# A head's products with v in two groups instead of three, and a pair's sums moved beside one of them

## The chip, the cores and the metric

The kernel runs on one core of one Trainium2 chip. The metric is the device time of one execution in microseconds (us). Before the change it is 525.54 us (median of three runs, 524.73 to 526.39).

## The reference

The program computes attention for 4 x 8 = 32 heads over 768 positions of width 64, with a mask: a key counts for a query only where both fall in the same bucket of 64 (the signs of six projections). The attention's output, seen as 3072 rows of width 512, goes through a soft mixture of 8 experts with 4 slots each.

```python
mask = q_bucket[:, :, :, None] == k_bucket[:, :, None, :]
scores = np.where(mask, scale * np.matmul(q, k.transpose(0, 1, 3, 2)), -1000000000.0)
attn = np.exp(scores - np.max(scores, axis=-1, keepdims=True))
attn = attn / (np.sum(attn, axis=-1, keepdims=True) + 1e-09)
x = np.matmul(attn, v)                  # rows of 512 = 8 heads x 64
logits = x @ phi                        # 32 slots
# softmax over rows feeds slots, w1, relu, w2; softmax over slots mixes them back
```

## The kernel before

**The work of a head.** Each head's 768 keys are six blocks of 128. For one head the kernel does the following.

- `smax` (L360): twelve products of 96 rows (L370), of 512 or 256 columns, whose row maxima VectorE takes (L373, L376). The twelve products fill nine PSUM tiles `smx` in turn: product n = 0 fills the first, 1 and 2 share the second, 3 the third, 4 the fourth, 5 and 6 the fifth, 7 the sixth, 8 the seventh, 9 and 10 the eighth, 11 the ninth. There are two buffers for them (L239), so a tile can be written once the maximum of the tile two before it has been taken. Here they are called M0 to M8.
- `shift` and `shift_rows` (L378, L389): three small VectorE steps make the shift from the maxima, TensorE transposes it (L404), ScalarE copies it (L407), and a DMA puts it into a row of the head's operands.
- `scores` (L411): twelve pairs of products (L421) into three PSUM buffers `st`, and an exponential on ScalarE (L425) into one of three tiles `pt`, one for each two blocks of keys.
- `acc` (L427): GpSimd adds up the exponentials of a head (L432, L438) for the sums.
- `av` (L440): the products with v. One call handles two blocks, with two halves of the columns side by side in the array, each 64 columns wide. One call is 4 products, which appear as 8 matmul records (L449). The third call of a head is followed by ScalarE's copy of the result to `avs` (L453).

**The work of a pair of heads.** `pair_sum` (L456) sums `acc` over the partitions with four products 32 columns wide (8 records, L461), and ScalarE copies the result to `sm` (L464). `pair_turn` (L492) transposes `sm` on TensorE (three transposes, L496); VectorE copies and inverts a small part (L498, L499). `pair_rec` (L466) inverts `sm` in place, a third at a time, on VectorE (L468); it overwrites what `pair_turn` reads, so it comes behind it. `pair_log` (L470) makes logits (8 records, L476), `pair_add` (L480) scales and adds them on VectorE (L488, L490), `pair_x` (L501) transposes and scales `avs` (L511, L513). On every second head VectorE also makes the low parts of the next pair's operands (`split_lo`, L292, two subtractions) and thresholds its bits (L321).

**What sets the order.** The order of the program is written out by hand. Every step gets a place on a line of slots, six slots a head, by the numbers in `WHEN` and `FIRST` (L45 to L113); the steps are sorted by it (L793) and written out in that order. Each engine runs its own instructions in the order in which they were written out. `pair_sum` of a pair has the number 16.448 counted from the start of the pair's first head, so it falls into the even head that comes after the pair. `s0` is the start of head h, `x` is 0 for even heads and 1 for odd ones.

Heads overlap: while the scores of head h run, the maxima of heads h + 1 and h + 2 are taken.

Of the kernel before, what the change touches and what calls it, by code (L numbers as in the profile page):

```python
# [17 lines left out]
BH = B * H  # L18
# [26 lines left out]
WHEN = {'load': -23.456,  # L45
 'bits': -14.465,
 'split_hi': -14.035,
 'split_lo': [-13.1, -12.626],
 'spread': [[-12.12, -11.747, -10.749, -7.5], [-12.05, -10.773, -10.639, -11.794]],
 'load_v': [-1.88, -1.85],  # L50
 'smax': [[-8.153, -7.646, -7.592, -7.407, -6.31, -6.263, -5.991, -5.086, -4.829, -4.442, -4.009, -3.019],
          [-7.926, -7.769, -7.645, -6.916, -6.247, -6.159, -6.133, -5.32, -4.829, -3.608, -3.608, -3.119]],
 'scores': [[-0.175, 0.609, 1.069, 1.557, 1.767, 2.599, 2.628, 3.37, 4.446, 4.862, 5.118, 5.577],
# [1 line left out]
 'shift': [-2.471, -2.398],  # L55
 'shift_rows': [-2.151, -1.917],
 'acc': [[5.646, 6.72, 8.258], [5.625, 6.02, 9.329]],
 'av': [[3.513, 6.554, 6.938], [3.513, 5.087, 6.68]],
 'pair_sum': 16.448,
 'pair_turn': 18.256,  # L60
 'pair_rec': [18.379, 18.389, 18.942],
 'pair_log': 18.557,
 'pair_x': [22.815, 24.33],
 'pair_add': 19.89,
# [83 lines left out]
def lsh_attention_soft_moe(  # L148
# [566 lines left out]
    def at(when, f, *args):  # L715
        key = (f.__name__, *(a for a in args if isinstance(a, int)))
        plan.append((FIRST.get(key, when), len(plan), (f, *args)))
# [10 lines left out]
    for h in range(BH):  # L728
        s0, x = NT * h, h % 2
        if x == 0:  # L730
            if h > 0:
                at(s0 + WHEN["load"], load, h)
            at(s0 + WHEN["bits"], bits, h)
            at(s0 + WHEN["split_hi"], split_hi, h)
            for n in range(2):
                at(s0 + WHEN["split_lo"][n], split_lo, h, n)
        for n, f in enumerate((spread_y, spread_bits, spread_l, spread_x)):
            at(s0 + WHEN["spread"][x][n], f, h)
        at(s0 + WHEN["load_v"][x], load_v, h)
        for n in range(2 * NT):  # L740
            at(s0 + WHEN["smax"][x][n], smax, h, n // 2, n % 2)
            at(s0 + WHEN["scores"][x][n], scores, h, n // 2, n % 2)
        at(s0 + WHEN["shift"][x], shift, h)
        at(s0 + WHEN["shift_rows"][x], shift_rows, h)
        for j in range(NT // 2):
            lone = h == BH - 1 and j == NT // 2 - 1
            at(s0 + (5.725 if lone else WHEN["acc"][x][j]), acc, h, j)
            if lone:
                for n in range(2):
                    at(s0 + 5.85 + n, av, h, j, n)  # L750
            else:
                at(s0 + WHEN["av"][x][j], av, h, j)
        if x and h < BH - 1:
            p, p0 = h - 1, s0 - NT
            at(p0 + WHEN["pair_sum"], pair_sum, p)
            at(p0 + WHEN["pair_turn"], pair_turn, p)
            for n in range(3):
                at(p0 + WHEN["pair_rec"][n], pair_rec, p, n)
            at(p0 + WHEN["pair_log"], pair_log, p)
            at(p0 + WHEN["pair_x"][0], pair_x, p, (0, 1))  # L760
            at(p0 + WHEN["pair_x"][1], pair_x, p, (2,))
            at(p0 + WHEN["pair_add"], pair_add, p)
        if h % H == H - 1 and h < BH - 1:
            for f in (batch_both, batch_max, batch_exp, batch_turn, batch_scale, batch_slots, batch_weigh, batch_share):
                at(p0 + WHEN[f.__name__], f, h // H)
    last, h = NT * BH, BH - 1
# [243 lines left out]
```

## Time and profile before

| What | Value |
|---|---|
| Time, median of three runs | 525.54 us |
| Profiled execution, its own time | 524.46 us |
| Its span from first to last instruction | 522.4 us |
| Granted TensorE clock, mean | 0.987 |
| TensorE busy | 499.2 us (96%) |
| VectorE busy | 369.3 us (71%) |
| GpSimd busy | 326.8 us (63%) |
| ScalarE busy | 246.6 us (47%) |
| Products with v (L449), busy | 145.3 us in 768 records |
| Row maxima (L376 and L373), busy | 130.8 and 65.6 us in 192 and 96 instructions |

A row of a timeline gives the start in us, the length in us, the engine, the line, the operation, what is written and read, the shape and how many instructions are merged. PE is TensorE, PEld its weight loads, DVE VectorE, ACT ScalarE, POOL GpSimd, SP the DMA issuing engine. Idle time before an instruction and what ended it stand in brackets. Two neighbouring rows can overlap, since an instruction's record reaches into the next one's; the distance between two starts is the time that the first one holds its engine.

### The profile page before, as it was taken

Reading aid. Unit: us, or ns where it says so; the run is one execution under the profiler, and the core shown is the slowest. Engines: PE = TensorE matmul, PEld = TensorE weight load, DVE = VectorE, ACT = ScalarE, POOL = GpSimd, SP = SyncE. Lnnn points to the kernel's source line nnn. Section 1 sums busy time; section 2 is a strip of 40 time slices with the busy share of each in tenths; the row PEclk is TensorE's granted clock in tenths of the full one; section 3 lists DMA queues with packets and bytes.
Section 4 is the critical chain, followed back from the end, with each engine's and each line's share of the span. In section 5 each row is a group of like instructions: output and inputs, shape, how many; then the busy total and the mean of one; then the engine's idle time right before and its main releaser. Section 6 shows DMA issues by size and latency. Waiting matters only on the chain.

```text
span 522.4 us, 9095 instructions
## 1 busy us (share of the span) xinstructions
PE 499.2 (96%) x3164; PEld 284.3 (54%) x3164; DVE 369.3 (71%) x703; ACT 246.6 (47%) x463; POOL 326.8 (63%) x223
## 2 busy tenths in 40 slices
PE   7968999999999999999999999999999999999992
PEld 4544555555555555556554555565555555553562
DVE  6574877787878787777787788787777885464233
ACT  4144536464646454545454545454644545422232
POOL 9246767676739776767488785856588767411200
PEclk9789999999999999999999999999999999999998
DMA  5747475758585657575765757676636366879967
GB/s 126 188 98 188 116 196 173 193 168 197 169 197 168 178 143 203 152 210 143 217 149 167 183 175 178 188 181 182 146 101 154 73 156 234 319 286 352 410 275 293
DMA packets 39777, 99.59 MB, mean 191 GB/s; under 512 B 7458, under 2 KB 13732, under 8 KB 39732
## 3 DMA queue, kind: packets, MB, share of 16 engines
q1 hardware_dynamic: 39540, 98.94, 66.3%
q8 instruction: 25, 0.41, 0.3%
q14 instruction: 20, 0.16, 0.1%
q0 software_dynamic: 192, 0.08, 0.1%
HBM read 52.76 MB, written 6.29 MB: 113 GB/s over the span
## 4 chain that ended last, share of the span: by engine, by line
PE 70%; DVE 10%; SPq 7%; DMA 6%; POOL 2%; issue 2%; ACT 1%; DVEq 0%; ACTq 0%; POOLq 0%
PE st L421 20%; PE av L449 19%; PE smx L370 13%; SPq L296 7%; DMA XY<-bt 4%; PE qs L933 3%; DVE w L292 3%; PE qh L851 3%; DVE mx L376 3%; PE mi L461 2%; PE mi L476 2%; POOL acc L438 1%; PE mi L328 1%; DMA w<-w 1%; DMA XY<-w 1%
## 5 line engine op out<-in xcount | busy, mean ns | idle before, releaser
L438 POOL TENSOR_TENSOR acc<-acc,pt 128x768 f32<-128x768 f32 x125 | 238.8, 1911 | 39.4 <-ACT pt L425 27.1
L425 ACT ACTIVATE pt<-st 128x512 f32<-128x512 f32 x288 | 162.0, 595 | 97.2 <-PE st L421 90.8
L421 PE MATMUL st<-XY 128*128 128x512 f32 (+1 forms) x768 | 183.7, 347 | 0.0
L376 DVE TENSOR_REDUCE mx<-smx 128x1 f32<-128x512 f32 x192 | 130.8, 687 | 54.1 <-PE smx L370 53.8
L449 PE MATMUL av<-pt,v 128*64 128x384 f32 x768 | 145.3, 499 | 0.0
L370 PE MATMUL smx<-XY 96*128 96x512 f32 (+1 forms) x384 | 126.6, 375 | 9.9 <-DVE mx L376 5.4
L421 PEld LDWEIGHTS st<-XY 128*128 128x128 f32 x768 | 123.7, 191 | 21.1 <-issue 10.6
L370 PEld LDWEIGHTS smx<-XY 96*128 96x128 f32 x384 | 70.1, 191 | 74.4 <-DVE mx L376 26.1
L432 POOL TENSOR_TENSOR acc<-pt 128x768 f32<-128x768 f32 x32 | 58.6, 1830 | 63.8 <-ACT pt L425 63.8
L449 PEld LDWEIGHTS av<-pt,v 128*64 128x64 f32 x768 | 46.5, 136 | 62.7 <-issue 57.5
L373 DVE TENSOR_REDUCE mx<-smx 128x2 f32<-128x512 f32 x96 | 65.6, 683 | 4.3 <-PE smx L370 4.1
L292 DVE TENSOR_TENSOR w<-raw,w 128x768 fp32r<-128x768 f32 x30 | 41.2, 1373 | 3.7 <-ACT w L288 3.7
L468 DVE RECIPROCAL sm<-sm 128x128 f32<-128x128 f32 x45 | 39.6, 910 | 0.0
L288 ACT CAST w<-raw 128x768 fp32r<-128x768 f32 x32 | 25.1, 831 | 19.5 <-DMA XY<-w 9.7
L453 ACT COPY avs<-av 128x384 f32<-128x384 f32 x32 | 15.3, 478 | 37.2 <-PE av L449 37.2
L407 ACT CAST mr<-mi 12x128 fp32r<-12x128 f32 x31 | 7.9, 255 | 49.2 <-PE mi L404 44.6
L321 DVE TENSOR_SCALAR bt<-mi,con 128x384 fp32r<-128x384 f32 x15 | 10.1, 677 | 25.3 <-DMA XY<-bt 9.6
L607 POOL TENSOR_TENSOR dl<-lacc,dl 64x384 f32<-64x384 f32 x3 | 3.0, 999 | 25.6 <-ACT dl L606 25.6
L513 DVE TENSOR_TENSOR xq<-mi,r 128x256 f32<-128x256 f32 x45 | 17.3, 412 | 0.4 <-PE mi L511 0.4
L328 PE MATMUL mi<-raw,pb 128*32 128x384 f32 x128 | 15.2, 517 | 0.1
L933 PE MATMUL qs<-w 128*32 128x256 f32 x232 | 15.2, 382 | 0.0
L511 PE MATMUL mi<-ident,avs 128*128 128x128 f32 x90 | 14.8, 273 | 0.0
(173 smaller groups left out, 339.4 us busy)
## 6 DMA issues: line engine op xcount, KB each, us to landing
w<-w SPq DMA_DIRECT2D x61, 512.0 KB
XY<-w SPq DMA_DIRECT2D x63, 384.0 KB
raw<-qk SPq DMA_DIRECT2D x32, 384.0 KB
XY<-w SPq DMA_DIRECT2D x64, 192.0 KB
v<-vt SPq DMA_DIRECT2D x32, 192.0 KB
out<-w SPq DMA_DIRECT2D x12, 512.0 KB
xq<-w SPq DMA_DIRECT2D x3, 512.0 KB
XY<-bt SPq DMA_DIRECT2D x62, 19.5 KB
```

The source lines that it names most:

```text
L292: (nc.vector if h else nc.gpsimd).tensor_tensor(out=w[:, 2 * x + 1], in0=st[h]["raw"][:, x], in1=w[:, 2 * x], op=ALU.subtract)
L296: eng.dma_start(out=dst.bitcast(F32), in_=src.bitcast(F32))
L370: nc.tensor.matmul(pt[:, o:o + b - a], s["Y"][0:96, 0, t * P:(t + 1) * P], s["Y"][0:96, 1, a:b], start=True, stop=True)
L373: nc.vector.tensor_reduce(out=mx[:, n - 1:n + 1], in_=pt.rearrange("p (a x) -> p a x", a=2), axis=AX.X, op=ALU.max)
L376: nc.vector.reduce_max(out=mx[:, n:n + 1], in_=pt, axis=AX.X)
L421: nc.tensor.matmul(pt[:, o:o + b - a], x[:, 1, i * P:(i + 1) * P], x[:, 0, a:b], start=first, stop=not first)
L425: nc.scalar.activation(s["P", i // 2][:, 512 * u:512 * u + 512], pt, AF.Exp, scale=D ** -0.5)
L432: nc.gpsimd.tensor_tensor(out=s["acc"], in0=pr[:, 0:S], in1=pr[:, S:2 * S], op=ALU.add)
L438: eng.tensor_tensor(out=s["acc"], in0=s["acc"], in1=pr[:, a * S:(a + 1) * S], op=ALU.add)
L449: nc.tensor.matmul(s["av"][64 * c:64 * c + 64, 0:HC], s["v"][:, i, :], pr[:, o + c * HC:o + (c + 1) * HC], start=(i == 0), stop=(i == NT - 1))
L468: nc.vector.reciprocal(out=rs[:, k * P:(k + 1) * P], in_=rs[:, k * P:(k + 1) * P])
L933: nc.tensor.matmul(po[32 * j:32 * j + 32], hTs[g][:, f, 32 * j:32 * j + 32], wt[1, x, 2 * g + f // 4, j][:, (f % 4) * HM:(f % 4 + 1) * HM] ...
```

## The change

The second and the third call of `av` of a head now stand directly behind each other, in even heads at the place of the former second call and in odd heads at the place of the former third, so 8 + 8 records become 16. The last head keeps its former numbers. `pair_sum` moves from the middle of an even head's score products to the place directly ahead of this group of 16; `pair_log` stands directly behind it, as it did behind the former second call. `pair_turn` moves from ahead of the second call to behind the first score products of the next head, and the three parts of `pair_rec` move behind it: the first ahead of the maximum of M5, the second and the third between the maxima of M5 and M6.

```diff
- 'av': [[3.513, 6.554, 6.938], [3.513, 5.087, 6.68]],
- 'pair_sum': 16.448,
- 'pair_turn': 18.256,
- 'pair_rec': [18.379, 18.389, 18.942],
+ 'av': [[3.513, 6.55, 6.555], [3.513, 6.67, 6.68]],
+ 'pair_sum': 18.5,
+ 'pair_turn': 18.9,
+ 'pair_rec': [18.91, 18.92, 18.95],
...
-                at(s0 + WHEN["av"][x][j], av, h, j)
+                at(s0 + (WHEN["av"][x][j] if h < BH - 1 else (3.513, 5.087)[j]), av, h, j)
```

The order on TensorE around the changed places, worked out from the numbers (`n` is the product of `smax`):

```
even head, before: scores, pair_sum, n=3, scores, n=4, n=5, n=6, pair_turn, av 2nd, pair_log, scores,
                   n=7, av 3rd, n=8, scores, n=9, scores, n=10, scores, n=11
even head, after:  scores, n=3, scores, n=4, n=5, n=6, pair_sum, av 2nd and 3rd, pair_log, scores,
                   pair_turn, n=7, n=8, scores, n=9, scores, n=10, scores, n=11
odd head, before:  n=3, av 2nd, n=4, scores, n=5, n=6, pair_x, scores, av 3rd, n=7
odd head, after:   n=3, n=4, scores, n=5, n=6, pair_x, scores, av 2nd and 3rd, n=7
```

On VectorE in the even head it was M4, turn, rec, rec, M5, rec, M6, add, M7, M8 and becomes M4, turn, rec, M5, rec, rec, M6, add, M7, M8 (the turn now a longer way behind M4). In the odd head VectorE's order stays as it was.

## The prediction

> **What bounds the kernel now.** I read the page first, then the busy time of one pair of heads, then the timelines of TensorE and VectorE through that pair, and last who waits for whom.
>
> ```profile
> span 522.4 us, 9095 instructions
> PE 499.2 (96%) x3164; PEld 284.3 (54%) x3164; DVE 369.3 (71%) x703; ACT 246.6 (47%) x463; POOL 326.8 (63%) x223
> ```
>
> TensorE looks like the whole bound. The middle of the kernel is 15 pairs of heads of about one length; one is cut out here by two starts of `pair_sum`. The columns are the stretch, its length, and the busy time of PE, PEld, DVE, ACT and POOL.
>
> ```profile
> 225.66:251.83 26.17, 26.17 (x157) 15.21 (x156) 20.21 (x38) 13.70 (x25) 18.91 (x11) 1.00 0.67 182
> ```
>
> TensorE has no gap in this pair, and the clock is fully granted. VectorE has 26.17 - 20.21 = 6.0 us to spare. That is little for an engine that TensorE leans on through only two buffers of maxima, so it matters where those 6.0 us lie. Here is TensorE's order through the even head, with what the change touches:
>
> ```profile
> 225.10 0.63 PE L421 MATMUL st<-XY 128*128 128x512 f32 x2
> 225.66 0.85 PE L461 MATMUL mi<-acc,ones 128*32 128x384 f32 x8
> 226.44 0.50 PE L370 MATMUL smx<-XY 96*128 96x512 f32 x1
> 226.78 1.10 PE L421 MATMUL st<-XY 128*128 128x256 f32 x6
> ...
> 228.19 0.49 PE L496 MATMUL mi<-ident,sm 128*128 128x128 f32 x3
> 228.61 1.51 PE L449 MATMUL av<-pt,v 128*64 128x384 f32 x8
> 230.05 0.85 PE L476 MATMUL mi<-avs,phs 64*32 64x384 f32 x8
> 230.83 0.73 PE L421 MATMUL st<-XY 128*128 128x512 f32 x2
> 231.40 0.40 PE L370 MATMUL smx<-XY 96*128 96x512 f32 x1
> 231.73 1.51 PE L449 MATMUL av<-pt,v 128*64 128x384 f32 x8
> 233.18 0.50 PE L370 MATMUL smx<-XY 96*128 96x512 f32 x1
> 233.51 0.63 PE L421 MATMUL st<-XY 128*128 128x256 f32 x4
> 233.99 0.28 PE L370 MATMUL smx<-XY 96*128 96x256 f32 x1
> ```
>
> The product n = 7 is at 231.40, n = 8 at 233.18 and n = 9 at 233.99. VectorE in the same stretch:
>
> ```profile
> 224.95 0.69 DVE L376 TENSOR_REDUCE mx<-smx 128x1 f32<-128x512 f32 x1 [0.95 <-PE smx L370]
> ...
> 229.36 0.16 DVE L498 COPY r<-mi 128x12 f32<-128x12 f32 x1
> ...
> 229.70 1.71 DVE L468 RECIPROCAL sm<-sm 128x128 f32<-128x128 f32 x2
> 231.84 0.69 DVE L376 TENSOR_REDUCE mx<-smx 128x1 f32<-128x512 f32 x1 [0.44 <-PE smx L370]
> 232.45 0.94 DVE L468 RECIPROCAL sm<-sm 128x128 f32<-128x128 f32 x1
> 233.71 0.69 DVE L376 TENSOR_REDUCE mx<-smx 128x1 f32<-128x512 f32 x1 [0.32 <-PE smx L370]
> 234.32 0.55 DVE L488 TENSOR_TENSOR sm<-mi,sm 128x384 f32<-128x384 f32 x1
> ...
> 235.38 0.68 DVE L373 TENSOR_REDUCE mx<-smx 128x2 f32<-128x512 f32 x1
> ...
> 236.79 0.17 DVE L382 TENSOR_REDUCE m<-mx 128x6 f32<-128x12 f32 x1
> ...
> 237.41 0.17 DVE L385 SCALAR_TENSOR_TENSOR mz<-m,mz 128x6 f32<-128x6 f32 x1
> ```
>
> The reader is to see that the copy of the turn and two reciprocals (229.36 to 231.41) run while TensorE is in its second group with v and the logits (228.61 to 230.83), where no maxima come in. M5, at 231.84, finds VectorE idle.
>
> **The gain on TensorE.** What a separate group costs is read from the third call of an even head. From n = 7 to the scores behind n = 8 it is 233.51 - 231.40 = 2.11 us. Without the group, n = 7 and n = 8 follow each other: four 256-column products take 233.99 - 233.51 = 0.48, so a 512-column one takes 0.24 and two take 0.48. Taking it out saves 1.63. Putting it behind the second call costs four more pairs of records. Their step shows in the weight loads:
>
> ```profile
> 232.11 0.14 PEld L449 LDWEIGHTS av<-pt,v 128*64 128x64 f32 x2 [0.18 <-issue]
> 232.43 0.14 PEld L449 LDWEIGHTS av<-pt,v 128*64 128x64 f32 x2 [0.18 <-issue]
> ```
>
> The step from 232.11 to 232.43 is 0.32, so four are 1.29 and a group of 16 takes 1.44 + 1.29 = 2.73. The gain is 1.63 - 1.29 = 0.34, say 0.35. It is the same for an odd head. The loads have nothing running ahead of them at the edges of such a group; that is the 0.35.
>
> `pair_sum` taken out of its place: from the second score product (225.10 + 0.63 - 0.40 = 225.33) to 226.78 is 1.45, without it 0.48, so 0.97 is saved; it costs 230.83 - 230.05 = 0.78 for an equal group (L476) beside the long one. No row shows a 32-wide group ahead of a 64-wide one. The bound is 0 (it drains as between full-width products) to 0.20; L476, which starts 1.44 after its 64-wide neighbour, is the nearest row, and gives 0.19, which I take. Per pair this makes 0.35 + 0.35 + 0.19 = 0.89.
>
> The Trainium skill, "TensorEngine Tiling (Array Packing)", section "Tiling Modes", says that a change of the tiling mode drains the array, while a change of tile inside a mode does not. By that rule alone the kernel gets faster with each group merged; the rows agree with it on this much, and the rival below carries it.
>
> **What it does to the maxima, even head.** I write TensorE's new order with the same steps.
>
> - n = 3 would follow at 225.33 + 0.24 = 225.57, but needs the buffer of M0, whose maximum ends at 224.95 + 0.69 = 225.64. The way in the other direction, from the end of n = 7 (231.40 + 0.40) to the start of M5 (231.84), is 0.04; I take 0.05. So n = 3 is at 225.69 and 0.12 of the gain is gone. What follows up to n = 6 lies 0.86 earlier than before.
> - `pair_sum` starts at 228.19 - 0.86 + 0.09 = 227.42 (0.09 is the edge: three transposes hold TensorE for 0.49 less the 0.16 by which the last record reaches into the next, as 0.40 less 0.24 of a 512-column product, so 0.33, and 228.61 - 228.19 is 0.42). The long group is at 228.20, `pair_log` at 230.93, the scores at 231.71, `pair_turn` 0.57 later (231.40 - 230.83) at 232.28, n = 7 at 232.61, n = 8 at 232.85, n = 9 in order at 233.57. Up to here TensorE is 233.99 - 233.57 = 0.42 ahead.
> - VectorE has M4 behind it before 229.36 - 0.86 = 228.5 (the copy came behind M4 then), and **waits for the turn some 4 us**. The copy comes at 232.28 + 0.49 + 0.04 = 232.81. The first reciprocal is 0.34 later, 233.15. How long one holds the engine is bounded by 1.71 - 0.94 = 0.77 (two, less a whole record) and 0.94 (a whole record); I take 0.82, nearer to the first, since the two do stand behind each other there.
> - M5 starts at 233.97 and ends at 234.66. n = 9 uses its buffer: it starts at 234.71, **a stall of 1.14**. Behind it in TensorE's order stand all scores, so nothing fills the gap.
> - The second and third reciprocals start at 234.58 (0.61 behind M5, as 232.45 - 231.84) and 235.40, M6 at 236.22, ending 236.91. n = 11 needs it; in order it would come 1.64 after n = 9 (rows below), 236.35. It comes at 236.96: **0.61** more.
> - The add starts at 236.83, M7 1.06 later at 237.89, the shift 1.41 later at 239.30, ending 0.79 later at 240.09. Its transpose on TensorE would be 3.01 behind n = 11, at 239.97; it comes at 240.14: **0.17** more.
>
> Against the 238.64 of the next rows the pair is 1.50 late: 1.92 of stalls less 0.42.
>
> **Odd head.** TensorE, then VectorE, from n = 11 of the even head on:
>
> ```profile
> 235.63 0.40 PE L370 MATMUL smx<-XY 96*128 96x512 f32 x1
> ...
> 238.64 0.28 PE L404 MATMUL mi<-ident,mz 128*12 128x128 f32 x1
> ...
> 241.09 0.39 PE L370 MATMUL smx<-XY 96*128 96x512 f32 x1
> 241.41 1.51 PE L449 MATMUL av<-pt,v 128*64 128x384 f32 x8
> 242.85 0.50 PE L370 MATMUL smx<-XY 96*128 96x512 f32 x1
> 243.18 0.64 PE L421 MATMUL st<-XY 128*128 128x512 f32 x2
> 243.66 0.41 PE L370 MATMUL smx<-XY 96*128 96x256 f32 x2
> ...
> 244.45 1.51 PE L449 MATMUL av<-pt,v 128*64 128x384 f32 x8
> 245.89 0.50 PE L370 MATMUL smx<-XY 96*128 96x512 f32 x1
> ```
>
> ```profile
> 241.53 0.95 DVE L292 TENSOR_TENSOR w<-raw,w 128x768 fp32r<-128x768 f32 x1
> 242.40 0.68 DVE L376 TENSOR_REDUCE mx<-smx 128x1 f32<-128x512 f32 x1
> ```
>
> The group at 241.41 stands exactly over `split_lo` and M2. Without it n = 5, which needs M2's buffer, would come at 241.09 + 0.24 + 0.24 + 0.48 = 242.05, but M2 ends at 243.08: n = 5 at 243.13, **a stall of 1.08**. The long group starts 0.79 later at 243.92, n = 7 follows 2.73 later at 246.65, against 245.89: **0.76 late**. No work of VectorE has gone, so the edge saved is smaller than the cover lost. The bounds are -0.35 (M2 in time) and +1.29 (n = 5 already waited for M2 before; then only the longer group counts).
>
> What else moves costs nothing: the copies on ScalarE (L464, L453) stand in a stretch where no exponential is due, since TensorE makes no scores in the long group; with that cover gone they delay one exponential by their own length, on an engine busy 13.70 of 26.17, with three score buffers in between. The tile `pt` of the former second call of an odd head is held longer, but its next writer is an exponential that comes behind the long group in TensorE's order anyway. No DMA is moved, and nothing on GpSimd's or SP's queue.
>
> **The sum.** Per pair 1.50 + 0.76 = 2.26. Fourteen pairs have both the maxima and the `split_lo` (the last ones have none left): 31.6 us. The merges without maxima beside them (head 0, the last sums with head 30, head 29) give 0.35 + 0.54 + 0.35 = 1.2 back. Some pairs already wait for a DMA behind the shift (total, times, longest):
>
> ```profile
> DVE bt L321 <- DMA XY<-bt: 9.6, 5, 2.3
> ```
>
> In these five a later TensorE waits less; with 0.6 each, an estimate from 1.50 of lateness against a wait of 1.9, that gives 2.9 back. 31.6 - 1.2 - 2.9 = 27.5, so 524.46 + 27.5 = 552 for the profiled execution. The median of the runs lies 1.1 above it: **553 us**.
>
> **Rivals.**
>
> - *TensorE is the bound and VectorE keeps up* (the drain rule at work): 31 merges at 0.35 and 15 sums at 0.19 save 13.7, giving 512 us. For it: 96% against 71% busy. Against it: the two queues in order, above. It would need M5 to be reduced ahead of the first reciprocal, or by 233.5, and M2 by 242.0. 0.07.
> - *Only one half stalls.* If the reciprocals were hidden, 14 x (0.76 - 0.42) - 1.2 = 3.6, giving 529; if only the even head stalls, 14 x (1.50 - 0.35) - 1.2 = 15, giving 540. 0.09.
> - *Both halves cost their upper bounds.* 1.29 in the odd head, and in the even one 2.0, if the steps behind each other on VectorE don't overlap by the 0.08 each (five or six steps): 14 x 3.3 = 46, giving 571. The pairs at a batch's end, with more on VectorE, point that way. 0.09.
> - *Loss and gain cancel* (within 0.3%, about what a measurement of this kernel can tell from no change): no mechanism of its own, 0.03.
>
> **How the numbers follow.** The forecast, some 540 to 566, has 0.72. The range of 538 to 570 leaves out the fast rival, the first half-case and the far end. Faster 0.07, same 0.03, slower 0.90.
>
> **What would show it.** Right: the copy of the turn (L498) with about 4 us idle ahead of it, ended by L496, in each pair; TensorE's loads at L370 waiting for maxima (L376) some 30 to 45 us longer in all; groups of 16 at L449 with 2.73 from start to next start; a pair 28.4 us long instead of 26.17. Wrong: no wait of n = 9 behind M5, or M2 done before n = 5 comes; then the time falls towards 512.

## The result and the profile after

The changed kernel takes 569.36 us (median of four runs, 567.82 to 570.1) against 525.96 us for the kernel before: a ratio of 1.086, with a 95% interval of 1.082 to 1.091. It is 43 us slower. The forecast was slower by 27.5 us, 553 us, with a range up to 570; the ratio times the 525.54 us of the prediction is 571, so the time lies at the far edge of the range and, by the ratio, just outside it.

The head of the page of the changed kernel, its clock row and its chain by engine and by line:

```profile
span 567.2 us, 9096 instructions
PE 506.3 (89%) x3164; PEld 294.6 (52%) x3164; DVE 379.0 (67%) x703; ACT 247.7 (44%) x463; POOL 331.8 (58%) x223
...
PEclk9879999999998999999979999999979999999997
...
PE 62%; DVE 26%; DMA 6%; SPq 1%; issue 1%; ACT 1%; DVEq 0%; ACTq 0%
PE av L449 21%; PE st L421 14%; PE smx L370 10%; DVE mx L376 6%; DVE sm L468 6%; DMA XY<-mr 3%; DVE w L292 3%; PE qs L933 3%; PE qh L851 3%; PE mi L461 2%; PE mi L476 2%; DVE mx L373 2%; DVE mz L383 2%; DVE lacc L490 1%; DVE xq L513 1%
```

TensorE fell from 96% busy to 89%, and VectorE now holds 26% of the chain that ends last. The clock row has three dips in the middle, at the 13th, 21st and 30th slice, that the row of before does not have. Who waited for whom in the changed kernel (total in us, times, longest):

```profile
DVE r L498 <- PE mi L496: 66.5, 15, 7.4
...
PE smx L370 <- DVE mx L376: 40.6, 43, 4.0
```

VectorE waits for the turn in all 15 pairs, and TensorE stands still for maxima, 40.6 us in all. Before, the second row had 5.4 us. Now the busy time by pair: the first and the last row are pairs in which a batch is closed, the middle one is an ordinary pair (columns as in the prediction; the tenth number, ahead of the DMA share, is the granted clock):

```profile
150.76:186.43 35.67, 31.29 (x171) 17.59 (x170) 24.39 (x46) 15.66 (x31) 18.71 (x13) 0.90 0.49 134
...
215.19:244.13 28.94, 26.32 (x157) 15.56 (x156) 21.48 (x38) 13.70 (x26) 19.48 (x11) 1.00 0.62 166
...
273.07:309.00 35.93, 31.82 (x172) 17.62 (x171) 24.62 (x46) 15.85 (x32) 18.98 (x15) 0.90 0.49 133
```

and a pair that closes a batch in the kernel before:

```profile
251.83:281.13 29.30, 28.89 (x171) 15.74 (x170) 23.72 (x46) 15.40 (x31) 19.12 (x15) 1.00 0.63 163
```

An ordinary pair went from 26.17 to 28.94; the forecast was 28.4. A pair that closes a batch went from 29.30 to 35.93, by 6.6 us, where the forecast took the 2.26 of the others. There are three such pairs, of 29.25, 29.30 and 29.39 us before and of 35.67, 35.93 and 36.09 after, and they are most of what the forecast lacks: 3 x (6.6 - 2.3) = 13 of the 17 us between the 27.5 forecast and the 44.8 by which the span grew.

TensorE in an ordinary pair, at the places that the prediction worked out:

```profile
220.05 0.49 PE L496 MATMUL mi<-ident,sm 128*128 128x128 f32 x3
220.30 0.71 PE L370 MATMUL smx<-XY 96*128 96x512 f32 x2
220.85 0.64 PE L421 MATMUL st<-XY 128*128 128x256 f32 x4
222.42 0.39 PE L370 MATMUL smx<-XY 96*128 96x256 f32 x1 [0.94 <-DVE mx L376]
...
224.63 0.50 PE L370 MATMUL smx<-XY 96*128 96x512 f32 x1 [0.32 <-DVE mx L376]
...
228.24 0.27 PE L404 MATMUL mi<-ident,mz 128*12 128x128 f32 x1 [0.42 <-DVE mz L385]
...
232.72 0.50 PE L370 MATMUL smx<-XY 96*128 96x256 f32 x2 [0.94 <-DVE mx L376]
...
233.61 2.80 PE L449 MATMUL av<-pt,v 128*64 128x384 f32 x16
236.34 0.50 PE L370 MATMUL smx<-XY 96*128 96x512 f32 x1
```

and VectorE:

```profile
220.58 0.17 DVE L498 COPY r<-mi 128x12 f32<-128x12 f32 x1 [4.22 <-PE mi L496]
...
220.93 0.89 DVE L468 RECIPROCAL sm<-sm 128x128 f32<-128x128 f32 x1
221.74 0.63 DVE L376 TENSOR_REDUCE mx<-smx 128x1 f32<-128x512 f32 x1
222.28 1.75 DVE L468 RECIPROCAL sm<-sm 128x128 f32<-128x128 f32 x2
223.95 0.63 DVE L376 TENSOR_REDUCE mx<-smx 128x1 f32<-128x512 f32 x1
...
225.07 1.21 DVE L490 TENSOR_TENSOR lacc<-lacc,sm 128x384 f32<-128x384 f32 x1
```

The reader sees all four stalls of the forecast at their places: n = 9 behind M5, n = 11 behind M6, the shift's transpose behind VectorE, and n = 5 of the odd head behind M2. The long group takes 236.34 - 233.61 = 2.73, as worked out. One thing was not in the walk: the second add, L490, took 1.21 us instead of 0.56. It ended at 226.28, 0.41 us behind the end of a sum of GpSimd; an experiment below takes that up:

```profile
224.04 1.83 POOL L432 TENSOR_TENSOR acc<-pt 128x768 f32<-128x768 f32 x1 [4.97 <-ACT pt L425]
```

A sign that the prediction named is met as well: TensorE's weight loads at L370 waited 60.8 us for the maxima of L376, against 26.1 before, 34.7 longer where 30 to 45 was forecast.

### The profile page after: what moved, and what is told of

Its sections match the earlier page's. It is cut to its first block, busy times and chain, and to the rows that moved or that the text cites. A ratio compares the mean times of both kernels' runs of the same rounds, so it can differ in the third digit from the quotient of the medians.

```text
span 567.2 us, 9096 instructions
## 1 busy us (share of the span) xinstructions
PE 506.3 (89%) x3164; PEld 294.6 (52%) x3164; DVE 379.0 (67%) x703; ACT 247.7 (44%) x463; POOL 331.8 (58%) x223
## 4 chain that ended last, share of the span: by engine, by line
PE 62%; DVE 26%; DMA 6%; SPq 1%; issue 1%; ACT 1%; DVEq 0%; ACTq 0%
PE av L449 21%; PE st L421 14%; PE smx L370 10%; DVE mx L376 6%; DVE sm L468 6%; DMA XY<-mr 3%; DVE w L292 3%; PE qs L933 3%; PE qh L851 3%; PE mi L461 2%; PE mi L476 2%; DVE mx L373 2%; DVE mz L383 2%; DVE lacc L490 1%; DVE xq L513 1%
## 5 line engine op out<-in xcount | busy, mean ns | idle before, releaser
L438 POOL TENSOR_TENSOR acc<-acc,pt 128x768 f32<-128x768 f32 x125 | 243.9, 1952 | 32.0 <-ACT pt L425 19.1
L376 DVE TENSOR_REDUCE mx<-smx 128x1 f32<-128x512 f32 x192 | 128.8, 679 | 51.1 <-PE smx L370 50.5
L370 PE MATMUL smx<-XY 96*128 96x512 f32 (+1 forms) x384 | 124.2, 383 | 42.5 <-DVE mx L376 40.6
L449 PE MATMUL av<-pt,v 128*64 128x384 f32 x768 | 145.1, 514 | 0.0
L370 PEld LDWEIGHTS smx<-XY 96*128 96x128 f32 x384 | 69.2, 194 | 92.5 <-DVE mx L376 60.8
L449 PEld LDWEIGHTS av<-pt,v 128*64 128x64 f32 x768 | 51.3, 142 | 73.9 <-issue 64.6
L453 ACT COPY avs<-av 128x384 f32<-128x384 f32 x32 | 15.3, 479 | 89.9 <-PE av L449 89.9
L292 DVE TENSOR_TENSOR w<-raw,w 128x768 fp32r<-128x768 f32 x30 | 45.8, 1527 | 3.9 <-ACT w L288 3.5
L498 DVE COPY r<-mi 128x12 f32<-128x12 f32 x15 | 2.6, 171 | 66.5 <-PE mi L496 66.5
L468 DVE RECIPROCAL sm<-sm 128x128 f32<-128x128 f32 x45 | 39.5, 908 | 0.0
L328 PE MATMUL mi<-raw,pb 128*32 128x384 f32 x128 | 14.8, 503 | 0.4 <-DMA raw<-qk 0.4
```

The costliest lines, as they stand in the source:

```text
L292: (nc.vector if h else nc.gpsimd).tensor_tensor(out=w[:, 2 * x + 1], in0=st[h]["raw"][:, x], in1=w[:, 2 * x], op=ALU.subtract)
L370: nc.tensor.matmul(pt[:, o:o + b - a], s["Y"][0:96, 0, t * P:(t + 1) * P], s["Y"][0:96, 1, a:b], start=True, stop=True)
L376: nc.vector.reduce_max(out=mx[:, n:n + 1], in_=pt, axis=AX.X)
L438: eng.tensor_tensor(out=s["acc"], in0=s["acc"], in1=pr[:, a * S:(a + 1) * S], op=ALU.add)
L449: nc.tensor.matmul(s["av"][64 * c:64 * c + 64, 0:HC], s["v"][:, i, :], pr[:, o + c * HC:o + (c + 1) * HC], start=(i == 0), stop=(i == NT - 1))
L468: nc.vector.reciprocal(out=rs[:, k * P:(k + 1) * P], in_=rs[:, k * P:(k + 1) * P])
```

## The experiments

In the diffs, a line of `av` has the numbers of the even heads first and those of the odd heads second. Eleven kernels ran, each beside the kernel before on the same chip.

**The odd heads' merge alone.** Against the kernel before:

```diff
- 'av': [[3.513, 6.554, 6.938], [3.513, 5.087, 6.68]],
+ 'av': [[3.513, 6.554, 6.938], [3.513, 6.67, 6.68]],
```

with the last head's numbers kept, as in the change.

> Only the odd heads' second group with v is moved behind to the third; the even heads and the pair's sums stay as before. Theory (the group covered VectorE's subtraction and M2): each normal pair is some 0.8 us longer, so 10 x 0.8 = 8, and in the three pairs at a batch's end, where M2 is later still, 1.3 to 4 us each with or without a spell of half clock: 534 to 546 us, some 538. Rival (edges of the group are what counts): 15 x 0.35 less, 520 us.

Measured: 541.53 us, ratio 1.027 (1.023 to 1.032). An ordinary pair is 27.21 us long, 1.0 longer, the three pairs that close a batch 30.50, 34.07 and 34.10:

```profile
229.03:256.24 27.21, 26.48 (x157) 15.14 (x156) 21.63 (x38) 13.61 (x25) 18.89 (x11) 1.00 0.67 175
256.24:290.31 34.07, 30.62 (x171) 16.76 (x170) 24.95 (x46) 15.75 (x31) 19.22 (x15) 0.95 0.54 141
```

The cover lost costs more than the edge saved, and the edge theory, which wanted 520, is out for this half. The clock of 0.95 in the second row shows half-rate time with this half of the change alone; the first of the three, of 30.50 us, has a clock of 1.00.

**The even heads' part alone.** Against the changed kernel:

```diff
- 'av': [[3.513, 6.55, 6.555], [3.513, 6.67, 6.68]],
+ 'av': [[3.513, 6.55, 6.555], [3.513, 5.087, 6.68]],
```

> Only the even heads' part of the change: the long group, the pair's sums ahead of it, the turn and the reciprocals behind it; odd heads as before. Theory (VectorE idles through the long group and then has the reciprocals ahead of M5 and M6): 1.5 to 2.0 us a pair in 14 pairs, so 546 to 553 us, and no spell of half clock in the pairs at a batch's end, since the second group of the odd head covers the subtraction there again. Rival (the spells come from the even head's lateness): the three spells stay, and the time is above 557 us.

Measured: 547.82 us, ratio 1.041 (1.037 to 1.044). An ordinary pair takes 28.10, one that closes a batch 31.72, both at a granted clock of 1.00. So this half costs 21.6 us and brings no half-rate time; the odd half alone cost 15.3. Together they make 36.9, the change 43.4. By the spans of the profiled executions it is 25.6 and 16.9, together 42.5 of 44.8, so the halves nearly add up. One part of the rest is that the change has half-rate time in all three pairs that close a batch, and the odd half alone in two.

**The even heads' merge without the move of the sums.** Against the kernel before:

```diff
- 'av': [[3.513, 6.554, 6.938], [3.513, 5.087, 6.68]],
+ 'av': [[3.513, 6.55, 6.555], [3.513, 5.087, 6.68]],
```

> Only the even heads' third group is moved up behind the second; the pair's sums, turn and reciprocals keep the places of before. Theory (the loss comes from where the turn and the reciprocals stand, not from the length of the group): 16 edges at 0.35 are saved and n = 9 waits some 0.2 for M5, since n = 7 and n = 8 then stand together: 525.5 - 5.6 + 3 = 523 us, 520 to 525. Rival (a long group by itself starves VectorE of maxima): at least 1 us a pair, 540 us or more.

Measured: 533.89 us, ratio 1.013 (1.010 to 1.016). Neither theory met it. It is 14 us less than with the moved sums, so most of the even half's loss does come from where the sums, the turn and the reciprocals stand (this run does not tell the three apart); but the gain did not come. All engines in an ordinary pair of this run (first TensorE, then VectorE, then GpSimd):

```profile
212.92 0.85 PE L328 MATMUL mi<-raw,pb 128*32 128x384 f32 x8
214.78 0.28 PE L404 MATMUL mi<-ident,mz 128*12 128x128 f32 x1 [1.00 <-DVE mz L385]
```

```profile
210.21 0.54 DVE L488 TENSOR_TENSOR sm<-mi,sm 128x384 f32<-128x384 f32 x1
210.79 2.04 DVE L490 TENSOR_TENSOR lacc<-lacc,sm 128x384 f32<-128x384 f32 x1
```

```profile
210.58 1.83 POOL L432 TENSOR_TENSOR acc<-pt 128x768 f32<-128x768 f32 x1 [3.55 <-ACT pt L425]
```

TensorE reaches `bits` (L328) 12.20 us after `pair_sum`, as before, and then waits 1.00 for the shift. VectorE's add of two SBUF operands began 0.21 after GpSimd's sum of two SBUF operands and ended 0.42 after it (212.83 against 212.41): by these times it stood still while GpSimd ran. In the kernel before, the same add ended 0.06 us ahead of GpSimd's sum:

```profile
234.90 0.56 DVE L490 TENSOR_TENSOR lacc<-lacc,sm 128x384 f32<-128x384 f32 x1
```

```profile
235.52 1.83 POOL L432 TENSOR_TENSOR acc<-pt 128x768 f32<-128x768 f32 x1 [3.55 <-ACT pt L425]
```

Within this run the add took 2.02 to 2.04 us in seven pairs; there the transpose of the shift came 14.04 to 14.06 us behind `pair_sum`. In the seven others, where it took 0.56 or where the first pair of a batch has no such add, it came 12.96 to 12.99 behind. That is 1.08 us in each of seven pairs, 7.6 us in all, about the loss of 7.7 by the medians. The mean of L490, eleven times, before and in this run:

```profile
L490 DVE TENSOR_TENSOR lacc<-lacc,sm 128x384 f32<-128x384 f32 x11 | 6.4, 582 | 0.4
```

```profile
L490 DVE TENSOR_TENSOR lacc<-lacc,sm 128x384 f32<-128x384 f32 x11 | 16.4, 1493 | 0.4
```

The Trainium skill, "SBUF — State Buffer", section "SBUF: two separate sides", says that VectorE and GpSimd take a shared pair of ports in turn, each for a whole instruction, where VectorE reads two SBUF operands. The rows agree: 2.04 us against 0.56, and the end just behind GpSimd's.

**The same without that add.** Against the kernel of the last run:

```diff
-        if g:
-            nc.vector.tensor_tensor(out=lacc_of[b], in0=lacc_of[b], in1=dst, op=ALU.add)
```

> The run with the bare even merge, without the second add of pair_add (L490): a batch's logits hold only the last product, the adding up over its pairs is left out. There that add took 1493 ns as a mean of 11 instead of 582, since it falls under GpSimd's sum, and the transpose of the shift waited 1.00 us for what stands behind it. Theory (GpSimd's sum holds the add up and this is the whole loss of the bare merge): a pair falls from 27.2 to 25.9 to 26.2, and the time to 519 to 524 us. Rival (the loss comes from the long group, whatever VectorE does): 531 us or more.

Measured: 524.69 us, ratio 0.997 (0.994 to 1.001): 9 us less than with the add, and 0.7 above the upper end of what was expected. So the add under GpSimd's sum accounts for the loss of the bare merge. What the kernel before would take without this add was not measured; there the add took 582 ns as a mean, so it was hardly held. It did not become a gain, though. Pairs of 26.1 to 26.8 alternate with pairs of 27.2 to 27.6, and in the longer ones n = 0 of the odd head waits for a DMA:

```profile
240.67 0.47 PE L370 MATMUL smx<-XY 96*128 96x512 f32 x1 [1.08 <-DMA XY<-mr]
```

**The changed kernel without the reciprocals.** Against the changed kernel, `pair_rec` (L468) is left out for all pairs:

```diff
+        st[h]["rs"] = sm
...
-                at(p0 + WHEN["pair_rec"][n], pair_rec, p, n)
+                if n < 0:
+                    at(p0 + WHEN["pair_rec"][n], pair_rec, p, n)
```

> The changed kernel without the three reciprocals of a pair's sums: the inversion of the sums is left out, so the logits are scaled with the sums themselves. Theory (the reciprocals behind the late turn hold M5 and M6 up): the stalls of n = 9 and n = 11 fall from 0.94 and 0.32 idle to some 0.1 and nothing, 1.5 to 1.9 us a pair, 25 us less than the changed kernel: 539 to 548 us; less still if the half-clock spells go too. Rival (the wait for the turn itself is the loss, whatever stands behind it): not more than 0.3 us a pair less, 565 us.

Measured: 537.19 us (median of four, 536.24 to 547.40), 32 less than the changed kernel. The stall of n = 11 is gone, and n = 9 comes some 0.3 late, without a wait in its row:

```profile
211.79 0.39 PE L370 MATMUL smx<-XY 96*128 96x256 f32 x1
```

An ordinary pair takes 27.1 to 27.8. The wait for the turn itself is as long as in the changed kernel, 66.5 us in 15 times, so it is what stands behind the turn that costs. In the profile half of what is gained, 16 of 32.6 us, comes from the three pairs that close a batch: they take 30.6 at a clock of 1.00, so the half-rate spells went too.

**The former place in three odd heads.** Against the changed kernel, heads 9, 17 and 25 keep their second group where it was:

```diff
-                at(s0 + (WHEN["av"][x][j] if h < BH - 1 else (3.513, 5.087)[j]), av, h, j)
+                at(s0 + (WHEN["av"][x][j] if h < BH - 1 and h not in (9, 17, 25) else (3.513, 5.087, 6.68)[j]), av, h, j)
```

> The changed kernel, but in heads 9, 17 and 25, the odd heads in which a batch is closed, the second group with v keeps its former place. Theory (there the stall ahead of n = 5 grows to some 3 us, and the clock then drops to half for 6.8 us): the three spells go, and the three long pairs fall from 36 to about 32: 12 us less, 557 us. Rival (the pairs at a batch's end are long for their additional VectorE work and not for this stall): 3 x 0.8 less, 567 us, and the spells stay.

Measured: 560.47 us, ratio 1.065 (1.061 to 1.069). That is 9 us less than the changed kernel by the medians and 11 by the ratios, which compare with the kernel before on the same chip. The pairs that close a batch fell to 31.72, at a clock of 1.00. Here is what happens in the changed kernel in such a pair, all engines but the weight loads:

```profile
289.34 2.28 DVE L292 TENSOR_TENSOR w<-raw,w 128x768 fp32r<-128x768 f32 x1
...
291.54 0.68 DVE L376 TENSOR_REDUCE mx<-smx 128x1 f32<-128x512 f32 x1
...
292.27 0.80 PE L370 MATMUL smx<-XY 96*128 96x256 f32 x2 [2.84 <-DVE mx L376]
...
294.49 4.75 PE L449 MATMUL av<-pt,v 128*64 128x384 f32 x16
```

The subtraction takes 2.28 us under GpSimd's sum instead of 0.95, M2 comes late, TensorE stands idle for 2.84 us (3.1 in the two other such pairs), and what follows runs at half the pace: the long group takes 4.75 instead of 2.80. The kernel before already had a trace of this: in the pair of 29.30 us the subtraction took 1.23 us, and n = 5 waited for M2 in spite of the group that covered it:

```profile
270.41 0.51 PE L370 MATMUL smx<-XY 96*128 96x256 f32 x2 [0.41 <-DVE mx L376]
```

The busy time and the clock (0.89 and 0.55 of full) in the stretches of the changed kernel:

```profile
289.30:292.30 3.00, 0.16 (x2) 0.03 (x1) 3.00 (x4) 2.33 (x6) 2.92 (x2) 0.89 0.94 285
292.30:299.20 6.90, 6.90 (x26) 3.66 (x26) 3.83 (x6) 0.84 (x2) 6.57 (x7) 0.55 0.48 149
```

**Filler in the same stall.** Against the changed kernel; the tile is read by nothing:

```diff
+    def fill(n):
+        pt = p_mi.tile([P, 512], F32, name="mi")
+        for _ in range(n):
+            nc.tensor.matmul(pt[0:32, 0:P], ones, ident, start=True, stop=True)
...
+        if h in (9, 17, 25):
+            at(s0 + 5.83, fill, 12)
```

> The changed kernel, with twelve additional small products into an unused tile in the stall ahead of n = 5 in heads 9, 17 and 25, so that TensorE is not idle there; nothing reads them. Theory (the idle time itself brings the half clock, and half of the loss of these pairs is the clock): the wait for M2 stays as a whole, the spells go, 6.1 us at half clock behind it become 3, so 3 x 3 = 9 us less: 560 us. Rival (the clock has another cause, or the loss is all stall): 569 us or a little more.

Measured: 561.51 us, ratio 1.069 (1.066 to 1.073), 7.9 less than the changed kernel by the medians, 8.9 by the ratios, from additional work alone:

```profile
270.44:303.41 32.97, 31.57 (x196) 18.62 (x195) 24.61 (x46) 15.48 (x32) 19.01 (x15) 1.00 0.53 145
```

The pair falls from 35.93 to 32.97 and its clock is 1.00. The filler takes the place of the idle time, and the long group behind it takes 2.80 us again (lines have other numbers in this kernel; L454 is L449):

```profile
286.82 2.81 PE L256 MATMUL mi<-ident,ones 128*32 128x128 f32 x24
...
290.86 2.80 PE L454 MATMUL av<-pt,v 128*64 128x384 f32 x16
```

VectorE is as busy as before (24.61 against 24.62 us) and the subtraction takes 2.29 again; the order of all else is the same. So the idle time brought the half rate, and it cost some 3 us in each of the three pairs. The Trainium skill, "TensorE: Matmul & The Clock Gate", section "Part 1: The HAM clock gate (the "warmup" mystery)", says that the array falls back to half its clock after an idle window of about 3.4 us. The trace agrees on the half rate; here an idle stretch of 2.84 us was enough. The length of one stretch is not the whole condition: in the run with VectorE's work placed anew, below, stretches of 1.63 to 1.69 us were followed by 3 us at 0.55 to 0.65, while stretches of 1.47 to 1.49 in the even heads' part alone, and one of 1.75 in the run with all merges, left the clock at 1.00. What else decides stays open.

**The odd heads' merge at the second place.** Against the kernel before:

```diff
- 'av': [[3.513, 6.554, 6.938], [3.513, 5.087, 6.68]],
+ 'av': [[3.513, 6.554, 6.938], [3.513, 5.087, 5.088]],
- 'pair_x': [22.815, 24.33],
+ 'pair_x': [22.815, 23.0],
```

> The kernel before, with the odd heads' third group moved up behind the second, where VectorE makes its subtraction, and the second part of pair_x moved ahead of the group, since the group's result takes the buffer that pair_x reads. Theory (the edge is worth 0.35 and the cover stays): 15 x 0.35 less, 520.5 us, 518 to 523. Rival (the exponentials of the last two blocks are not done so early, or VectorE lacks the cover at the former third place): 525 us or more.

Measured: 526.9 us, ratio 1.0045 (1.002 to 1.007). The group is 2.74 us long and the stall ahead of n = 5 does not come back, but in this pair n = 7 waits 0.29 for M3, whose subtraction takes 2.06 under GpSimd's sum. Such a wait of 0.17 to 0.62 us stands in eleven pairs, against one of 0.26 in the kernel before, so that as much is lost there as the edge of 0.35 would save. The way from the shift's transpose to n = 0 is the same as before, 0.58 to 0.93 us against 0.58 to 1.08.

**The even heads' merge with VectorE's work placed anew.** Against the bare even merge:

```diff
- 'pair_rec': [18.379, 18.389, 18.942],
- 'pair_add': 19.89,
+ 'pair_rec': [18.379, 18.389, 18.395],
+ 'pair_add': 18.95,
```

and the tenth number of the even heads' `smax` from -4.442 to -4.09.

> The bare even merge, with all three reciprocals under the long group and pair_add between M5 and M6, so that its adds are done before GpSimd begins, and n = 9 behind one more score product. Nothing is left out. Theory (the add was held up by GpSimd): the add is back at 0.56, and the time at 520 to 525 us. Rival (the next of VectorE's steps that reads memory falls under GpSimd's sum in its place, as the shift's L383 did with 1.80 us in the run of all merges): 529 to 535 us, with L383 longer.

Measured: 532.68 us, ratio 1.012 (1.008 to 1.017). The add is back at 558 ns, and the rival's case came: the shift's L383 went from 336 ns before to 718 as a mean, the hold-up came one step later. How much of the 532.68 us it explains is not shown. The profiled execution, of 537.74 us the longest of six, also shows n = 0 waiting 1.69 us for a DMA, with half-rate time behind it (the pair's clock is 0.94, its length 30.50), and half-rate time in the pairs that close a batch (0.95, 32.3):

```profile
215.39 0.47 PE L370 MATMUL smx<-XY 96*128 96x512 f32 x1 [1.69 <-DMA XY<-mr]
```

**All merges where VectorE has cover.** The last two kernels' numbers together, and `pair_sum` at 15.52, behind the even head's first group.

> The kernel before with all merges where VectorE has its cover: odd heads as in the run with the group moved up; even heads' third group up behind the second; the pair's sums behind the even head's first group instead of ahead of the long one; turn where it was and all three reciprocals behind it, so that they run under the long group; pair_add between M5 and M6, ahead of GpSimd's next sum; n = 9 one score product later. Theory (edges at 0.35, 0.35 and 0.19 to be saved, nothing lost): 13.7 us less, 512 us, 510 to 516. Rival (VectorE's order or GpSimd's hold on the memory port takes it back as in the run with the bare even merge): 521 us or more.

Measured: 540.9 us, ratio 1.030 (1.026 to 1.033), 29 us above what was expected. VectorE and GpSimd in one pair of it:

```profile
214.40 1.80 DVE L383 TENSOR_SCALAR mz<-m 128x6 f32<-128x6 f32 x1
```

```profile
214.35 3.73 POOL L438 TENSOR_TENSOR acc<-acc,pt 128x768 f32<-128x768 f32 x2
```

A step over six numbers a row takes 1.80 us since it began 0.05 after GpSimd's sum. Behind it, n = 0 waits 1.08 for a DMA.

**The sums behind the first group, alone.** Against the kernel before:

```diff
- 'pair_sum': 16.448,
+ 'pair_sum': 15.52,
```

> The kernel before with the pair's sums directly behind the even head's first group with v, and nothing else moved. Theory (an edge of 0.19 saved 15 times, no work of VectorE moved): 522 to 524 us. Rival (the stretch behind it becomes 0.1 to 0.2 earlier against VectorE and the DMAs and waits there instead): 525 to 527 us.

Measured: 536.24 us, ratio 1.019 (1.016 to 1.023): even the smallest edit made it slower, by more than the rival said. Five of the six executions took 535.86 to 537.44 us. The profile is of the sixth, 546.48 us, ten above them, so its waits can't be read as the cause of the others' 536: there n = 0 of an odd head waits 2.63 us for a DMA. Why this edit costs 9 us stays open.

No kernel of these beats the kernel before.

## Why the prediction was right and wrong

The direction and the mechanism held. **Even head:** VectorE waits 4.22 us for the turn (forecast some 4). From `pair_turn`, n = 9 comes 2.37 us later (forecast 2.43), n = 11 comes 4.58 later (4.68), the shift's transpose 8.19 later (7.86). The first two are met; the third is 0.33 over, since the add L490 took 1.21 us and not 0.56, and its wait is 0.42 where 0.17 was forecast. Leaving out the reciprocals took the stall of n = 11 away and left 0.3 of that of n = 9, with the turn as late as ever, which shows that the reciprocals at that place are the cause.

**Odd head:** from the transpose, n = 5 comes 4.48 later (forecast 243.13 - 238.64 = 4.49) and n = 7 8.10 later (8.01). The long group's 2.73 is exact.

**The pair:** 28.94 against a forecast of 28.4. Over the ten ordinary pairs that is some 5 us. The relief where a pair already waited for a DMA was right: pairs of 26.17 and of 26.87 before both take 28.8 to 29.0.

**The step that failed** is "Fourteen pairs have both the maxima and the `split_lo`: 31.6 us", that is 14 times one price, read from one ordinary pair. It rests on "15 pairs of heads of about one length", and that was misread: in the kernel before three of them already took 29.3 us, against 26.2 to 26.9. These three close a batch. There VectorE has more to do ahead of M2, the subtraction falls under GpSimd's sum, and TensorE is idle for 2.84 us where the forecast had 1.08; its clock then falls to half for what follows, a term that the forecast put at nothing. Such a pair costs 6.6 us and not 2.26. The filler puts some 3 us of this, 7.9 in all three, down to the clock; the other 3.7 is the stalls. The wait of 0.41 us of n = 5 in such a pair before was the condition of the prediction's own upper bound of 1.29 for the odd head. The prediction named these pairs only as a pointer in the rival of upper bounds. That rival's 571 us meets the number by luck: it charges 3.3 us to each of 14 pairs, and the runs show 2.8 in ordinary ones and 6.6 in three.

**The gain side** was right in its rows and wrong as an offer. A group of 16 does take 2.73 instead of two times 1.44. But in no run was an edge saved paid out as time: the runs that gave VectorE its cover back were at best equal. The rival of 512 us would have needed more than VectorE's order: the run that came nearest to its conditions took 540.9 us, with a step of VectorE held up beside GpSimd's sums and n = 0 waiting for a DMA. Whether these two are all that stood in its way was not tested.

## What to carry to other kernels

Before work that covers another engine is moved, write down what runs under it: here the products with v were the time in which VectorE could catch up, worth more than the 0.35 us of each edge. Price the odd periods by themselves, the ones that close a batch, and ask of every stall on TensorE, here from 1.6 us up, whether it also costs the clock. Where VectorE adds, subtracts or compares from SBUF to SBUF while GpSimd sums, look at which of the two begins first: here an add that began 0.21 us behind GpSimd's sum took 2.04 us, and one that began 0.62 ahead of it 0.56.

## What the runs showed of the hardware

- An idle stretch of 2.84 us on TensorE was followed by 6.9 us at 0.55 of the clock, and the same order with products in that stretch stayed at 1.00 (569.36 against 561.51 us). Stretches of 1.63 to 1.69 us were followed by half-rate time in one run, stretches of 1.47 to 1.49 and one of 1.75 in others were not.
- VectorE's add of two SBUF operands took 0.56 us ahead of GpSimd's sum and 2.04 us when GpSimd's sum began 0.21 us ahead of it; a threshold over 128 x 6 values took 1.80 us in the same way, 0.05 us behind the start of a sum. Not every step is held: the two reciprocals in place at 229.70 in the kernel before took 1.71 us while GpSimd summed (228.26 to 231.97), about what they take elsewhere (0.94 for one).
- The first product of a head (n = 0) waited for a DMA for up to 1.75 us in the run with all merges, 1.69 in the run with VectorE's work placed anew and 1.20 in the run without the add, against 0.33 once in the kernel before. Which of the queue's transfers is late, and why, stays open.
